# VectorE makes one GELU chunk in each of six groups of the first MoE as well

## The chip, the cores and the metric

The kernel runs on one core of a Trainium2 chip, as one launch. The metric is device time in microseconds (us). The profile names the core's engines PE (TensorE, matmuls; PEld are its weight loads), ACT (ScalarE), DVE (VectorE), POOL (GpSimd) and SP (SyncE, which issues DMAs).

## The reference

Attention over spatially pooled keys, followed by a feed-forward layer ("MoE" in the code) with a quick GELU:

```python
kv_pool = kv.reshape(B, H // r, r, W // r, r, C).mean(axis=(2, 4))
kv_flat = kv_pool.reshape(B, -1, C) @ w_sr
k = v = kv_flat
scale = 1.0 / np.sqrt(C)
s = scale * (q @ k.transpose(0, 2, 1))
s = s - s.max(-1, keepdims=True)
a = np.exp(s)
a /= a.sum(-1, keepdims=True) + 1e-09
x = (a @ v).reshape(B * S, D)
h = x @ w_in
g = h * (1.0 / (1.0 + np.exp(-1.702 * h)))
out = g @ w_out
```

q is 4 x 12288 x 128, kv is 4 x 384 x 32 x 128, r is 4, so each batch has 768 pooled keys. w_in is 128 x 2048, w_out 2048 x 128. All 49152 tokens pass through both parts.

## The kernel before, in words

**Tiles.** The tokens are cut into 96 groups of 512 (NG = 96). In attention a group has JC = 6 *chunks*, one for each 128 keys; in the MoE it has FCH = 16 chunks, one for each 128 hidden units. A chunk is a 128 x 512 tile of exponentials (attention) or of GELU values (MoE).

**Fill and drain.** Each chunk is made in a *fill* and used up in a *drain*. A fill is one matmul with 512 columns into a PSUM bank (L350 in attention, L596 in the MoE). ScalarE then turns three banks at a time, a *triple* of 1536 columns, into bf16 values (L352 Exp, L598 GELU) in a large SBUF tile `ag` of 102 chunk slots, handed out in frames of K = 3. A drain of attention is four times one matmul of 129 columns (L363: the values and the sum of weights). A drain of the MoE is one matmul of 512 columns (L606), sixteen of which add up in one bank. Because `ag` holds 102 chunks, the drains may run far behind the fills.

**Banks.** Six of the eight PSUM banks hold two triples by turns. The other two, 6 and 7, are accumulators (`acc()`) which attention's outputs, a MoE group's outputs and single extra fills take by turns. VectorE empties them: a reciprocal and a multiply for attention (L386, L389, into `x`), a transpose for a MoE group (L617, after which SP writes the output, L619).

**Rounds.** There are R = 2 rounds: attention for groups 0 to 47, MoE for groups 0 to 47 (here "the first MoE"), attention for 48 to 95, MoE for 48 to 95 ("the second MoE"). In the trace the first MoE's fills run from 140 to 485 us, its drains from 158 to 501 us. `x` holds one round; it is turned around by way of DRAM (`put_away`, `bring_back`, on SP's queue).

**Chunks that VectorE makes.** Some chunks bypass ScalarE. TensorE fills them singly into an accumulator bank (`early_fill`, L415 for attention and L409 for the MoE), and VectorE evaluates the function by a polynomial, instruction by instruction (`early_exp`, L431 to L444; `lent_gelu`, L453 to L475). There are three lists:

- `rolling`: single exponentials of attention, groups 10, 38 and 44 in the first round and 57, 63, ... in the second;
- `early`: all 24 exponentials of groups 48 to 51, made during the first MoE, from its group 12 on (`low`), into the lowest slots of `ag`;
- `lent`: the last chunk (number 15) of 17 groups of the second MoE.

Chunks of `rolling` and `lent` go into the small tile `aside` with K = 3 slots, taken by turns in the order in which the chunks are made. `early_todo` is that order; only its head is ever started. `raw`, the scratch for a lent chunk, is a slot of the pool of transposed queries (`qpool`, four buffers).

**The order of the work** is written out by a planner in Python, from L793 on. It keeps a clock of TensorE (`now`, in units of one 512-column matmul), one of VectorE (`dve`) and the expected ends of ScalarE's triples (`end`). Between one fill and the next it places, in this order: a step of a VectorE chunk, if VectorE's clock is not far ahead (`dve <= now + 2.0`, L807); a new VectorE chunk (L810), not during the last drains of a MoE group (`near`) and not unless `early_fits`; else drains, until the next fill is due. `early_fits` lets a lent chunk start when a group at most two before its own is being filled (L490) and when its slot of `aside` has been used up. A MoE group's drains don't start before its lent chunk is made, by the planner's clock (L840, L841):

```python
or (kind == "m" and first_of and (i, FCH - 1) in lent
    and made.get((i, FCH - 1), 1e9) > now + 1.0)
```

The order so fixed is each engine's program; the waits on the chip are semaphores.

**Background work.** `background(i)` runs when attention group i is first filled, `background_moe(g)` likewise for the MoE. They issue query loads (`load_qT`, by the dictionary `TURN`: group -> query tile), transposes of x, and the keys of batches 2 and 3, which are summed by accumulating DMAs on POOL's queue (`add_kv`, L173, each behind a `gate()` that VectorE sets) and then pass through VectorE and TensorE (`use_kv`; L179, L186, L193, L201) at groups 12 and 14, and 34 and 36, of the first MoE.

Of the kernel before, what the change touches and what calls it, by code (L numbers as in the profile page):

```python
# [7 lines left out]
F32 = mybir.dt.float32  # L8
F32R = mybir.dt.float32r
I32 = mybir.dt.int32  # L10
BF = mybir.dt.bfloat16
# [13 lines left out]
def kernel(  # L25
# [10 lines left out]
    FCH = d_ff // 128  # L36
    scale = 1.0 / (C ** 0.5)
    G = 512
    SG = 4 * G
    NG = B * N // G  # L40
    NS = NG // 4
    GB = NG // B
    SB = NS // B
    K = 3
# [24 lines left out]
    qpool = ctx.enter_context(tc.tile_pool(name="qpool", bufs=4))  # L69
# [15 lines left out]
    def acc(key=None):  # L85

        nonlocal last_acc
        last_acc = next_acc()
        turns.append(last_acc)
        turns.remove(last_acc)  # L90
        if key:
            closes[last_acc] = key
        return banks[:, last_acc, :]
# [24 lines left out]
    kv_tiles, kv_sums, pooled, pTs, kTs, vs = {}, {}, {}, {}, {}, {}  # L118
# [86 lines left out]
    qTs = {}  # L205
# [6 lines left out]
    def load_qT(s):  # L212
        qTs[s] = qpool.tile([128, 1, SG], BF, name="qT")
        nc.vector.memset(qTs[s][:, 0, 0:1], 0.0)
        nc.sync.dma_start_transpose(out=qTs[s], in_=q_bf[s * SG:(s + 1) * SG, :])


    QS = 3
# [7 lines left out]
    turned = set()  # L226
# [46 lines left out]
    for m in range(0, 128, 32):  # L273
        p = slice(m, m + 32)
# [30 lines left out]
    low = 0  # L305
# [23 lines left out]

    early = range(NG // R, NG // R + EARLY)  # L330
    rolling = [(i, JC - 1) for i in [10, *range(38, NG // R, 6), *range(57, 90, 6)]]
    lent = [(g, FCH - 1) for g in range(52, 94) if g % 5 in (2, 4)]
    aside = agpool.tile([128, K, 512], BF, name="aside")

    def weights(c):
        if c[0] == "a" and c[1] in early:
            return ag[:, (c[1] - early[0]) * JC + c[2], :]
        if c[0] == "a" and c[1:] in rolling:
            return aside[:, rolling.index(c[1:]) % K, :]
        if c[0] == "m" and c[1:] in lent:  # L340
            return aside[:, (len(rolling) + lent.index(c[1:])) % K, :]
        return ag[:, slot_of[c], :]


# [56 lines left out]
    COEFFS = (1.0000001192092896, -0.6931469440460205, 0.24022120237350464, -0.05550713464617729, 0.009675541892647743, -0.001327647129073739)  # L401

    def early_fill(i, jc):
        nonlocal steps, raw
        ps = acc()
        if (i, jc) in lent:
            if raw is None:
                raw = qpool.tile([128, 1, SG], BF, name="qT")[:, 0, 0:2 * G].bitcast(F32)
            nc.tensor.matmul(ps, w_in_sb[:, jc * 128:(jc + 1) * 128],  # L409
                             x[:, i % (4 * XS) * G:(i % (4 * XS) + 1) * G], start=True, stop=True)  # L410
            steps = lent_gelu(ps, weights(("m", i, jc)))
            early_step()
            return
        rhs = qTs[i // 4][:, 0, (i % 4) * G:(i % 4 + 1) * G]
        nc.tensor.matmul(ps, kTs[i // GB][:, jc * 128:(jc + 1) * 128], rhs, start=True, stop=True)  # L415
        steps = early_exp(ps, weights(("a", i, jc)))
        early_step()

    def early_step():
        nonlocal steps  # L420
        on_dve(next(steps))
        if steps.gi_frame.f_locals["last"]:
            steps = None
            made[early_todo.pop(0)] = dve
# [23 lines left out]
    def lent_gelu(ps, out):  # L448
        last = False
        a = npool.tile([128, 512], F32, name="ea", bufs=1)  # L450
        b = npool.tile([128, 512], F32, name="eb", bufs=1)
        e = npool.tile([128, 512], I32, name="ee", bufs=1)
        nc.vector.tensor_scalar_mul(raw, ps, -1.702 / LN2)  # L453
        yield 3.5
        nc.vector.tensor_scalar(a, raw, -126.0, 127.0, MAX, MIN)
        yield 2.2
        nc.vector.tensor_scalar_add(b, a, MAGIC)
        yield 2.2
        nc.vector.tensor_scalar(e, b, MAGIC - 127.0, 2.0 ** 23, SUB, MUL)
        yield 2.2  # L460
        nc.vector.scalar_tensor_tensor(b, b, MAGIC, a, SUB, SUB)
        yield 3.5
        nc.vector.tensor_scalar_mul(a, b, COEFFS[5])
        yield 2.2
        for k in (4, 3, 2, 1):
            nc.vector.scalar_tensor_tensor(a, a, COEFFS[k], b, ADD, MUL)  # L466
            yield 3.5
        nc.vector.scalar_tensor_tensor(a, a, COEFFS[0], e.bitcast(F32), ADD, MUL)
        yield 3.5
        nc.vector.tensor_scalar_add(a, a, 1.0)  # L470
        yield 2.2
        for m in (0, 256):
            nc.vector.reciprocal(b[:, m:m + 256], a[:, m:m + 256])  # L473
            yield RECIPROCAL
        nc.vector.scalar_tensor_tensor(out, raw, -LN2 / 1.702, b, MUL, MUL)  # L475
        last = True
        yield 3.5

    raw = None
    made, used = {}, []  # L480
    steps, early_todo = None, [c for c in rolling if c[0] < early[0]]
    early_todo += [(i, jc) for i in early for jc in range(JC)]
    early_todo += [c for c in rolling if c[0] > early[-1]] + lent

    def early_fits(p, i, jc):
        if (i, jc) in rolling:
            group = seq[p][1][0][0] if seq[p][0] == "a" else seq[p][1][0][0] // (NG // R) * (NG // R) + NG // R - 1
            return (i // GB, jc) in vs and (i in turned or i // 4 in qTs and i // 4 - 1 <= group // 4 and i >= 4 * QS) and len(used) > rolling.index((i, jc)) - K
        if (i, jc) in lent:
            return seq[p][0] == "m" and seq[p][1][0][0] >= i - 2 and len(used) > len(rolling) + lent.index((i, jc)) - K  # L490
        return low and min(slot_of.values()) >= low and (2, JC - 1) in vs

    def early_waits(t):
# [12 lines left out]
    def bring_back(n, m):  # L506
        o = m * PART
        lo = n * XS * SG + o * T
        nc.sync.dma_start_transpose(out=x[:, o * T:(o + PART) * T].unsqueeze(1), in_=x_bf[lo:lo + PART * T, :])
# [6 lines left out]
    def gate():  # L516

        one = gate_tile[:, gates[0] % 8:gates[0] % 8 + 1]
        gates[0] += 1
        nc.vector.memset(one, 0.0)  # L520
        nc.gpsimd.memset(one, 0.0)  # L521

    TURN = {6: 3, 7: 4, 8: 5, 20: 6, 21: 7, 22: 8, 25: 9, 32: 10, 35: 11, 40: 12}
    CAST = {0: [5], 13: [6], 14: [7], 15: [8], 16: [9], 26: [10, 11], 27: [12]}
    CAST_MOE = {20: 13, 21: 14, 22: 15, 23: 16, 33: 17, 34: 18, 35: 19, 36: 20, 37: 21, 38: 22, 39: 23}

    def background(i):

        first_round = i < GB * 2
        s = TURN.get(i, NS) if first_round else i // 4 + 3 if i % 4 == 0 else NS  # L530
        if s < NS:
            load_qT(s)
        if i in CAST:
            gate()
            for s in CAST[i]:
                cast_q(s)
        if i in (10, 12):
            gate()
            for jc in range(i % 10 * 3 // 2, i % 10 * 3 // 2 + 3):
                load_chunk(1, jc)  # L540
        if 0 <= i - 16 < JC:
            extras.append((key_and_value, 1, i - 16))
        if 0 <= i - 15 < JC:
            extras.append((pool_chunk, 1, i - 15))
        if i in (28, 33, 38):
            put_away(0, (i - 28) // 5)
        if i in (31, 36, 41):
            bring_back(0, (i - 31) // 5)
        if i == 28:
            gate()  # L550
            nc.gpsimd.dma_start(out=w_in_sb, in_=moe_w_in)
        if i == 29:
            gate()
            nc.gpsimd.dma_start(out=w_out_sb, in_=moe_w_out.rearrange("(o p) c -> p o c", p=128))

    def background_moe(g):

        n, g = divmod(g, 4 * XS)
        m, odd = divmod(g - 9, 2)
        m += FIRST  # L560
        if n == 0 and FIRST <= m < RT // PART:
            (bring_back if odd else put_away)(n, m)
        g += n * 4 * XS
        nonlocal low
        if g == 12:
            low = EARLY * JC
            order[:] = [f for f in order if f >= low // K]
        if g in CAST_MOE:
            gate()
            cast_q(CAST_MOE[g])  # L570
        if g in (41, 42):
            load_qT(g - 28)
        if g == 43:
            background(early[0])
        for b, lo in ((2, 2), (3, 24)):
            if lo <= g < lo + 8:
                gate()
                add_kv(b, g - lo)
            if g in (lo + 10, lo + 12):
                use_kv(b, (g - lo - 10) // 2)  # L580
# [74 lines left out]
    seq, todo = [], []  # L655
    todo_early = [("a", t, a) for t in range(NT) for a in range(2) if (t // TS * TS + TS - 1) // 4 in early]
    for n in range(R):
        part = [c for c in chunks if c[0] // (NG // R) == n]
        while part:
            m = sizes.pop(0) if sizes else K  # L660
# [12 lines left out]
        while flat:  # L673
            m = K if len(flat) > sum(rest) else rest.pop(0)
# [83 lines left out]
    def on_dve(cost):  # L758
        nonlocal dve
        dve = max(dve, now + 1.0) + cost  # L760
# [36 lines left out]
    for n in range(len(seq)):  # L797
        fill(n + 2)
        jobs(n + 3)
        while True:  # L800
# [33 lines left out]
            kind, i, c = source[0]  # L834
# [21 lines left out]
            if kind == "a" and i // 4 in early:  # L856
                early_left -= 1
                if not early_left:
                    low = 0
# [33 lines left out]
```

## Time and profile before

| | |
|---|---|
| median of 3 runs | 948.41 us (948.23 to 948.77) |
| span of the profiled execution, first to last instruction | 946.7 us |
| ACT: idle in the whole span | 13 us (933.5 busy), most of it in the first 35 us |
| L598 ACTIVATE, 1536 columns | 1496 ns each, 501 of them |
| L596 and L606, 512 columns | 379 ns each by a modelled end |
| DVE busy, 160 to 240 us | 10.50 of 80 us |
| DVE busy, 240 to 480 us | 175.53 of 240 us |
| DVE busy, 640 to 920 us | 199.22 of 280 us |

The profile is of one execution; its span leaves out what lies before the first and after the last instruction. A line of a group reads: source line, engine, operation, tiles written and read, count, then busy time, mean length of one, and the idle time of the engine just before, with what ended it. Lengths overlap where an engine is pipelined: an ACTIVATE is recorded as 1496 ns long, while the next one starts earlier than that. The chain of waits is read from start, length, and what ran; consecutive instructions of a line are joined ("x3").

### The profile page before, as it was taken

The page shows a single profiled execution, that of the slowest core. Times are in us where ns is not written, and L with a number is a line of the kernel's source. Part 1 is how long each engine was busy: PE and PEld are TensorE (multiplying, and loading weights), DVE is VectorE, ACT ScalarE, POOL GpSimd, SP SyncE. Part 2 cuts the span into 40 slices and gives each one's busy share as a digit, 9 for nine tenths or more (in the row PEclk, how much of TensorE's full clock was granted, in tenths as well). Part 3 has the DMA queues.
Part 4 walks back from the last instruction along what each step waited for, and adds up shares of the span by engine and source line. Part 5 has one row for each costly group of instructions (what it writes and reads, how often), then busy time and mean ns, then how long its engine had stood idle before and what let it go on. Part 6 is the DMA issues. An engine that isn't in the chain of part 4 may idle for free.

```text
span 946.7 us, 15374 instructions
## 1 busy us (share of the span) xinstructions
PE 933.9 (99%) x6200; PEld 502.5 (53%) x6314; DVE 575.1 (61%) x1091; ACT 933.5 (99%) x709; POOL 66.5 (7%) x115
## 2 busy tenths in 40 slices
PE   8999999999999999999999999999999999999998
PEld 4677776444444444444446777744444444444444
DVE  5753653011678776667765765376767766777651
ACT  6999999999999999999999999999999999999998
POOL 3101001330000232000000000000000000000000
PEclk9999999999999999999999999999999999999999
DMA  9997943999867799865335683552222222222222
GB/s 210 195 207 168 181 92 52 130 163 170 164 117 114 119 147 119 127 99 87 56 58 105 138 170 84 119 123 42 36 39 40 38 41 34 44 34 45 34 45 46
DMA packets 372856, 95.46 MB, mean 101 GB/s; under 512 B 346720, under 2 KB 370400, under 8 KB 372320
## 3 DMA queue, kind: packets, MB, share of 16 engines
q1 hardware_dynamic: 344000, 62.36, 36.9%
q0 software_dynamic: 28512, 31.99, 22.3%
q8 instruction: 49, 0.80, 0.3%
q14 instruction: 23, 0.19, 0.1%
q10 hardware_dynamic: 272, 0.13, 0.0%
HBM read 52.49 MB, written 48.76 MB: 107 GB/s over the span
## 4 chain that ended last, share of the span: by engine, by line
PE 97%; ACT 1%; DMA 1%; issue 1%; DVE 0%; POOL 0%; POOLq 0%
PE banks L606 35%; PE banks L596 34%; PE banks L363 14%; PE banks L350 12%; ACT ag L352 1%; PE banks L415 1%; DMA x<-in_kv_dram 1%; PE banks L139 0%; PE banks L409 0%; PE banks L634 0%; PE banks L236 0%; POOL x L222 0%; PE banks L161 0%; PE banks L294 0%; PE banks L192 0%
## 5 line engine op out<-in xcount | busy, mean ns | idle before, releaser
L598 ACT ACTIVATE ag<-banks 128x1536 bf16<-128x1536 f32 (+1 forms) x509 | 681.1, 1489 | 0.0
L596 PE MATMUL banks<-x,w_in_sb 128*128 128x512 bf16 x1476 | 405.8, 379 | 1.7
L606 PE MATMUL banks<-ag,w_out_sb 128*128 128x512 bf16 x1477 | 402.6, 379 | 1.7
L352 ACT ACTIVATE ag<-banks 128x1536 bf16<-128x1536 f32 (+2 forms) x192 | 245.6, 1421 | 3.5 <-PE banks L236 2.3
L606 PEld LDWEIGHTS <-w_out_sb 128*128 128x128 bf16 x1520 | 148.3, 98 | 177.2 <-issue 0.2
L596 PEld LDWEIGHTS <-w_in_sb 128*128 128x128 bf16 x1519 | 147.1, 98 | 171.3 <-issue 0.7
L617 DVE STREAM_TRANSPOSE o_sb<-banks 128x512 f32<-128x512 f32 x95 | 68.1, 717 | 171.4 <-PE banks L606 166.9
L363 PEld LDWEIGHTS <-ag 128*128 128x128 bf16 x2268 | 145.5, 98 | 44.6 <-issue 0.3
L363 PE MATMUL banks<-v,ag 128*128 128x129 bf16 x2268 | 163.0, 220 | 0.2
L350 PE MATMUL banks<-qT,kT 128*128 128x512 bf16 x498 | 145.0, 379 | 3.5 <-ACT ag L352 0.5
L442 DVE SCALAR_TENSOR_TENSOR ea<-ea,eb 128x512 f32<-128x512 f32 x132 | 90.4, 685 | 3.7 <-DVE ea L442 0.7
L386 DVE RECIPROCAL rec<-banks 128x3 f32<-128x3 f32 x124 | 22.3, 180 | 85.3 <-PE banks L363 84.9
L389 DVE TENSOR_TENSOR x<-banks,rec 128x384 bf16<-128x384 f32 x124 | 69.1, 557 | 4.3
L350 PEld LDWEIGHTS <-kT 128*128 128x128 bf16 x543 | 45.8, 98 | 25.9 <-issue 2.0
L473 DVE RECIPROCAL eb<-ea 128x256 f32<-128x256 f32 x34 | 57.6, 1724 | 0.5
L466 DVE SCALAR_TENSOR_TENSOR ea<-ea,eb 128x512 f32<-128x512 f32 x68 | 46.5, 683 | 1.9
L173 POOL DMA_DIRECT2D kvs<-in_kv_dram x32 | 40.4, 1323 | 19.3 <-DMA kvs<-in_kv_dram 17.1
L431 DVE TENSOR_SCALAR ea<-banks 128x512 f32<-128x512 f32 x33 | 22.8, 692 | 29.6 <-PE banks L415 29.2
L521 POOL MEMSET gate_tile<- 1x1 f32 x38 | 3.4, 89 | 325.8 <-DVE gate_tile L520 325.8
L453 DVE TENSOR_SCALAR qT<-banks 128x512 f32<-128x512 f32 x17 | 11.8, 692 | 20.7 <-PE banks L409 20.6
L437 DVE SCALAR_TENSOR_TENSOR eb<-eb,ea 128x512 f32<-128x512 f32 x33 | 22.8, 691 | 0.9
L444 DVE SCALAR_TENSOR_TENSOR ag<-ea,ee 128x512 bf16<-128x512 f32 x24 | 16.6, 691 | 1.2
(83 smaller groups left out, 286.3 us busy)
## 6 DMA issues: line engine op xcount, KB each, us to landing
out_dram<-o_sb SPq DMA_DIRECT2D x380, 64.0 KB, 2.0
kvs<-in_kv_dram POOLq DMA_DIRECT2D x32, 384.0 KB, 6.3
q_bf<-in_q_dram POOLq DMA_DIRECT2D x21, 512.0 KB, 6.6
x_bf<-x SPq DMA_DIRECT2D x13, 768.0 KB, 5.6
x<-in_kv_dram POOLq DMA_DIRECT2D x11, 512.0 KB, 10.4
x_bf<-x SPq DMA_DIRECT2D x6, 384.0 KB, 4.6
x<-in_q_dram POOLq DMA_DIRECT2D x5, 256.0 KB, 15.3
x<-in_kv_dram SPq DMA_DIRECT2D x1, 1024.0 KB, 5.0
```

What stands on the lines that cost most here:

```text
L173: nc.gpsimd.dma_start(out=kv_sums[b][:, i2], in_=kv_p[b, i, w, :, i2], **({"accum_op": ADD} if n else {}))
L350: nc.tensor.matmul(ps[:, k, :], kTs[i // GB][:, jc * 128:(jc + 1) * 128], rhs, start=True, stop=True)
L352: nc.scalar.activation(place([("a",) + c for c in chunks]), ps, AF.Exp, scale=scale)
L363: nc.tensor.matmul(av_of[u][:, k * (C + 1):(k + 1) * (C + 1)], weights(("a", i, jc))[:, o:o + T], vs[i // GB][:, jc, 0:C + 1], start=(jc = ...
L389: nc.vector.tensor_tensor(to, ps[:, :, 0:C], rec.unsqueeze(2).broadcast_to([128, TS, C]), MUL)
L442: nc.vector.scalar_tensor_tensor(a, a, COEFFS[k], b, ADD, MUL)
L466: nc.vector.scalar_tensor_tensor(a, a, COEFFS[k], b, ADD, MUL)
L473: nc.vector.reciprocal(b[:, m:m + 256], a[:, m:m + 256])
L596: nc.tensor.matmul(ps[:, k, :], w_in_sb[:, fc * 128:(fc + 1) * 128], x[:, g % (4 * XS) * G:(g % (4 * XS) + 1) * G], start=True, stop=True)
L598: nc.scalar.activation(place([("m",) + c for c in chunks]), ps, AF.Gelu_apprx_sigmoid)
L606: nc.tensor.matmul(o_of[g], w_out_sb[:, fc, :], weights(("m", g, fc)), start=(fc == 0), stop=(fc == FCH - 1))
L617: nc.vector.transpose(o_sb, o_of.pop(g))
```

## The change

Six chunks are added to the front of `lent`: chunk 15 of groups 2, 4, 6, 8, 10 and 12 of the first MoE. They leave the triples of that MoE (762 chunks for ScalarE in place of 768) and are made in `early_todo` after the three `rolling` chunks of the first round and before the 24 `early` ones. The turns of `aside` get a list of their own, `turn`, in the same order. `raw` is now taken when attention group 40 is filled, given back at group 43 of the first MoE, and taken again for the second MoE; the load of query tile 12 moves from group 40 to group 42, which keeps the four buffers of `qpool` in step.

```diff
-    lent = [(g, FCH - 1) for g in range(52, 94) if g % 5 in (2, 4)]
+    lent = [(g, FCH - 1) for g in range(2, 13, 2)] + [(g, FCH - 1) for g in range(52, 94) if g % 5 in (2, 4)]
+    turn = [("a",) + c for c in rolling if c[0] < early[0]] + [("m",) + c for c in lent if c[0] < early[0]]
+    turn += [("a",) + c for c in rolling if c[0] > early[-1]] + [("m",) + c for c in lent if c[0] > early[-1]]
...
-        if c[0] == "a" and c[1:] in rolling:
-            return aside[:, rolling.index(c[1:]) % K, :]
-        if c[0] == "m" and c[1:] in lent:
-            return aside[:, (len(rolling) + lent.index(c[1:])) % K, :]
+        if c in turn:
+            return aside[:, turn.index(c) % K, :]
...
             if raw is None:
-                raw = qpool.tile([128, 1, SG], BF, name="qT")[:, 0, 0:2 * G].bitcast(F32)
+                new_raw()
...
+    def new_raw():
+        nonlocal raw
+        raw = qpool.tile([128, 1, SG], BF, name="qT")[:, 0, 0:2 * G].bitcast(F32)
...
+    early_todo += [c for c in lent if c[0] < early[0]]
     early_todo += [(i, jc) for i in early for jc in range(JC)]
-    early_todo += [c for c in rolling if c[0] > early[-1]] + lent
+    early_todo += [c for c in rolling + lent if c[0] > early[-1]]
...
-            return seq[p][0] == "m" and seq[p][1][0][0] >= i - 2 and len(used) > len(rolling) + lent.index((i, jc)) - K
+            return seq[p][0] == "m" and seq[p][1][0][0] >= i - 2 and len(used) > turn.index(("m", i, jc)) - K
...
-    TURN = {6: 3, 7: 4, 8: 5, 20: 6, 21: 7, 22: 8, 25: 9, 32: 10, 35: 11, 40: 12}
+    TURN = {6: 3, 7: 4, 8: 5, 20: 6, 21: 7, 22: 8, 25: 9, 32: 10, 35: 11, 42: 12}
...
+        if i == 40:
+            new_raw()
...
         if g == 43:
+            raw = None
             background(early[0])
```

More of the change, by code (lines that the diff above doesn't have):

```diff
@@ L403, in early_fill @@
     def early_fill(i, jc):
-        nonlocal steps, raw
+        nonlocal steps
         ps = acc()
@@ L487, in early_fits @@
             group = seq[p][1][0][0] if seq[p][0] == "a" else seq[p][1][0][0] // (NG // R) * (NG // R) + NG // R - 1
-            return (i // GB, jc) in vs and (i in turned or i // 4 in qTs and i // 4 - 1 <= group // 4 and i >= 4 * QS) and len(used) > rolling.index((i, jc)) - K
+            return (i // GB, jc) in vs and (i in turned or i // 4 in qTs and i // 4 - 1 <= group // 4 and i >= 4 * QS) and len(used) > turn.index(("a", i, jc)) - K
         if (i, jc) in lent:
-            return seq[p][0] == "m" and seq[p][1][0][0] >= i - 2 and len(used) > len(rolling) + lent.index((i, jc)) - K
+            return seq[p][0] == "m" and seq[p][1][0][0] >= i - 2 and len(used) > turn.index(("m", i, jc)) - K
         return low and min(slot_of.values()) >= low and (2, JC - 1) in vs
@@ L563, in background_moe @@
         g += n * 4 * XS
-        nonlocal low
+        nonlocal low, raw
         if g == 12:
```

## Prediction

> **What bounds the kernel now.** I read the page's busy shares first, then the groups of instructions, then the chain inside the first MoE, then the counts of weight loads by stretch, because the first two can't decide between TensorE and ScalarE. From the page:
>
> ```profile
> span 946.7 us, 15374 instructions
> ...
> PE 933.9 (99%) x6200; PEld 502.5 (53%) x6314; DVE 575.1 (61%) x1091; ACT 933.5 (99%) x709; POOL 66.5 (7%) x115
> ...
> L598 ACT ACTIVATE ag<-banks 128x1536 bf16<-128x1536 f32 (+1 forms) x509 | 681.1, 1489 | 0.0
> L596 PE MATMUL banks<-x,w_in_sb 128*128 128x512 bf16 x1476 | 405.8, 379 | 1.7
> L606 PE MATMUL banks<-ag,w_out_sb 128*128 128x512 bf16 x1477 | 402.6, 379 | 1.7
> ```
>
> ScalarE's GELU line (L598) has no idle time before it. TensorE's two MoE lines have 1.7 us each, but their 379 ns are modelled ends, so "busy" could hide a wait of some 160 ns before each matmul. Start times can't hide it. This is the chain of waits in a stretch of the first MoE:
>
> ```profile
> 163.40 0.65 PE banks L596 x3
> 164.04 0.65 PE banks L606 x3
> 164.69 0.65 PE banks L596 x3
> ...
> 166.63 0.86 PE banks L606 x4
> 167.50 0.65 PE banks L596 x3
> ...
> 171.38 0.65 PE banks L596 x3
> 172.03 0.86 PE banks L606 x4
> ```
>
> From 163.40 to 172.03 the unabridged chain holds 40 matmuls of 512 columns: 8.63 / 40 = 0.2158 us from start to start. Whether three or four drains (L606) stand between two fills (L596), it is the same spacing; a TensorE that waited for ScalarE would show gaps ahead of the fills. Now the count. Weight loads, one a matmul, in the window 160 to 240 us, where this change puts most of its work:
>
> ```profile
> L606 PEld LDWEIGHTS <-w_out_sb 128*128 128x128 bf16 x189 | 18.5, 98 | 22.3
> L596 PEld LDWEIGHTS <-w_in_sb 128*128 128x128 bf16 x180 | 17.5, 98 | 20.7
> L184 PEld LDWEIGHTS <-pooled 96*128 96x128 bf16 x4 | 0.3, 97 | 0.2
> L199 PEld LDWEIGHTS <-pT 128*128 128x128 bf16 x3 | 0.3, 98 | 0.2
> L192 PEld LDWEIGHTS <-w_sr_sb 128*128 128x128 bf16 x1 | 0.1, 98 | 0.1
> ```
>
> 369 x 0.2158 = 79.6 us and about 0.5 us for the eight small ones: 80.1 of 80 us. The same sum for 240 to 480 us (535 + 526 + 24 wide loads, 72 of the 129-column kind at 0.057, 24 small) gives 239.8 of 240, and for 640 to 920 us, in the second MoE with its lent chunks, (658 + 625 + 15) x 0.2158 = 280.1 of 280. Over the whole trace I added up by how much each step from one weight load to the next exceeds the usual one for its shape: after 60 us this comes to 0.65 us in all, no single step over 0.11 us. Before 60 us it is about 10 us, the start-up, which the change doesn't reach. So TensorE is full from 60 us to the last matmul. ScalarE is full as well, by the windows view:
>
> ```profile
> 160.00:240.00 80.00, 79.58 (x370) 36.51 (x377) 10.50 (x23) 80.00 (x61) 19.02 (x20) 1.00 1.09 151
> ...
> 640.00:920.00 280.00, 278.63 (x1273) 126.87 (x1298) 199.22 (x274) 280.00 (x210) 0.00 (x0) 1.00 0.25 39
> ```
>
> The columns are PE, PEld, DVE, ACT, POOL, then the granted clock (1.00). VectorE has 10.5 of 80 us of work where the new chunks go. ScalarE is at 80.00: two engines are saturated together, and freeing one of them frees nothing unless the other also gets less.
>
> **Part by part.** *Removed from ScalarE:* 6 chunks leave the triples of the first MoE, 768 - 6 = 762 = 254 triples in place of 256. From 158.72 us, 31 ACTIVATEs take 41.91 us: (41.91 - 1.50) / 30 = 1.347 us from one to the next, so ScalarE loses 2 x 1.347 = 2.69 us of work.
>
> *TensorE:* six fills move from L596 to the early fill's matmul, with the same weights, tokens and 512 columns, and the six drains stay. Its work changes by 0. Since TensorE is late everywhere, the 2.69 us turn into ScalarE waiting. All that could be won is the 0.65 us of stalls; I count 0, and keep -0.65 us as the end of the range.
>
> This is where the Trainium skill speaks for a gain. "Perfetto Trace Analysis" (Identifying the Most-Contended Engine) says to judge TensorE by the share of weight-load time and the others by occupancy; here that is 53% against ScalarE's 99%, so ScalarE would bound and the change would win its 2.69 us. "TensorE: Matmul & The Clock Gate" (Back-to-back issue gap) gives about 131 ns per 512-column matmul for a sustained stream; by that figure, as an estimate, TensorE would need 48 of the 80 us. This trace shows no 512-column step below 0.215 us, so I go by the trace.
>
> *VectorE:* one GELU chunk costs, by the rows of the second MoE, 0.692 (L453) + 4 x 0.427 (L455, L457, L459, L470) + 0.690 + 0.424 + 4 x 0.683 (L466) + 0.690 + 2 x 1.724 (L473) + 0.669 = 11.05 us. Six are 66 us. VectorE is idle for 69.5 us in 160 to 240 and 11.9 us in 140 to 160, so there is room, but little: the chunks come every second group. What hides them is the lead of fills over drains. Group 2 is filled from 155.4 us and its drain starts at 171.65 us; group 12 from 227.55 and 239.1. A chunk must be made before the planner lets its group's drain begin.
>
> The pace: in the second MoE a chunk takes 12.7 to 14.4 us from its first VectorE instruction to its last, 13.6 on average, with one or two evacuations (L617) inside, and 0.65 us more from its weight load. 14.3 us a chunk stands against two groups of drains, 2 x (239.07 - 158.27) / 12 = 13.47 us, so each chunk comes 0.8 us later against its group. The first may start when group 0 is filled, 140.3 us, and shares VectorE with the last attention normalisations until 158.8 us. An exponential in such company took 12.2 us, against 7.5 us in the MoE, 1.63 times as long. From 141.5 us: (158.3 - 141.5) / 1.63 = 10.3 of 13.6 us are done by 158.3, the rest by 162. That is 9.7 us before group 2's drain; five chunks later 9.7 - 5 x 0.83 = 5.5 us; the pooled keys of batch 2 (L179, L186, L193, L201) take 2.2 us of VectorE at 225 to 232 us, which leaves some 3.3 us for group 12. No drain is held: cost 0.
>
> *Small terms.* Each lent chunk borrows one of the two accumulator banks until L453 has read it. Of 17 such fills and 33 exponential fills in the trace, 7 show an extra step, 0.55 us together, the longest 0.108 us: six more cost 0 to 0.65 us; I take the mean, 0.55 us / 50 x 6, about 0.1 us. An evacuation may wait for a 1.72 us reciprocal, but the other bank has a whole group (6.7 us) to come free. ScalarE's pace beside a busy VectorE: 210 ACTIVATEs start in 280 us (1.333 us) in the second MoE, no slower. POOL's eight accumulating key loads wait for gates that VectorE sets; batch 3's loads have run beside a busy VectorE, and L179 waited for nothing there. The load of query tile 12 moves from group 40 to group 42: SP issued it at 118.45 us, then the transposed load of x at 122.56, then nothing until 165.47; its first reader is the exponential at 246.9 us. The order of the two swaps in an idle queue: cost 0. The 24 early exponentials start after the last lent chunk; they began at 246.9 us, after the keys of batch 2, and (12, 15) is made by about 236 us. If it were 3 us late, the last exponential, made at about 482 us, would still be before its drain at 487.08: cost 0, and if that cover were gone, a microsecond late is at most a microsecond.
>
> *Sum:* 946.7 + 0.1 = 946.8 us of span. The median, 948.41, lies 1.7 us above the span of the one profiled execution; I carry that over: **948.5 us**.
>
> **Rivals.** (A) *ScalarE is what bounds.* For it: no idle before L598, and 80.00 of 80. Against: the constant 0.2158 us with four drains in a row, and 80.1 us of matmuls in 80. It would give 948.4 - 2.7 = 945.7 us. Chance 0.03.
>
> (B) *A held drain, slower.* The planner doesn't open a group's drain until its lent chunk is made by its own VectorE clock. While it holds, TensorE only fills, 3 matmuls per 1.347 us where 6.24 fit: 52% of the hold is lost for good, since nothing later has slack. It decides from the point where the first chunk is made after 171.65 us, or a chunk takes over 13.47 + 9.7 / 5 = 15.4 us. If the first chunk starts only after the last normalisation (158.8), it is made at 173.1: held 1.5 us, then 0.83 more for each of five, and 2.2 for the keys: 7.8 us held, 4.1 lost: 952.5 us. For it: 14.3 against 13.47, and fills that allow no chunk to start in the last drains of a group. Against: the 17 chunks of the second MoE were made 10.1 us or more before their own drain, the last of sixteen, and so 3.6 us or more before their group's first. Chance 0.10.
>
> (C) *The order behind it.* The early exponentials slip past their drains at 487 us, or the shifted order puts a wait into the second half: 1 to 3 us, 951 us. Chance 0.03.
>
> That the chunks aren't moved can't be: they leave the triples' list, and would be missing.
>
> **The numbers.** Likeliest, 0.84: 948.5 us, own range 947.4 (stalls of 0.65 gone, 0.4 of scatter between runs) to 949.5 us. For 8 in 10 the range reaches into B and C up to 950.8 us. Within 0.2% (1.9 us, about what a measurement of this kernel can tell from no change) lies the likeliest case: 0.84. Faster 0.03 is A; slower 0.13 is B and C.
>
> **What would show it.** Right: in the changed profile the wide matmuls still start every 0.2158 us from 160 to 240 us; ScalarE has 2 activations fewer and idle time of about 2.7 us, ended by TensorE; VectorE's load in 160 to 240 rises from 10.5 to about 70 us; the lent drains come several us after L475. Wrong: fills with gaps ahead of them and runs of fills without drains between (B), late L363 drains around 490 us (C), or a span near 944 us with ScalarE still at 100% (A). What would make it wrong above all is a chunk slower than 15.4 us.

## The result and the profile after

The changed kernel takes 950.26 us (median of 18 runs, 950.15 to 950.52), the kernel before 948.56 us (18 runs, 948.18 to 948.80): a ratio of 1.0019, 95% interval 1.0012 to 1.0026. It is 1.7 us slower. That is inside the 1.9 us that the prediction counted as no change, but above the range of its likeliest case (947.4 to 949.5 us); only the part of the range that was added for the slower rivals B and C, up to 950.8 us, takes it in. The page of the changed kernel, whose lines from 419 on have moved (L596 is now L604, L606 is L614, L598 the activation is L606, L617 is L625):

```profile
span 948.4 us, 15584 instructions
...
PE 940.8 (99%) x6314; PEld 502.7 (53%) x6314; DVE 638.0 (67%) x1181; ACT 930.8 (98%) x707; POOL 67.0 (7%) x115
...
L606 ACT ACTIVATE ag<-banks 128x1536 bf16<-128x1536 f32 (+1 forms) x507 | 678.3, 1500 | 0.0
L604 PE MATMUL banks<-x,w_in_sb 128*128 128x512 bf16 x1513 | 409.3, 379 | 0.0
L614 PE MATMUL banks<-ag,w_out_sb 128*128 128x512 bf16 x1497 | 406.8, 379 | 0.0
```

ScalarE has two ACTIVATEs and 2.7 us of busy time less (930.8 against 933.5), VectorE 63 us more. The span grew by 1.7 us, from 946.7 to 948.4, as the medians did. TensorE's busy time can't be compared, since the profile of before had lost 114 matmul records and this one none; weight loads are 6314 in both. The windows view of the changed kernel (PE, PEld, DVE, ACT, POOL, clock):

```profile
160.00:240.00 80.00, 80.00 (x379) 36.40 (x377) 64.37 (x102) 80.00 (x61) 19.40 (x21) 1.00 1.07 153
...
640.00:920.00 280.00, 280.00 (x1298) 126.76 (x1296) 198.41 (x274) 280.00 (x210) 0.00 (x0) 1.00 0.26 39
```

VectorE went from 10.50 to 64.37 us between 160 and 240, where about 70 was forecast; TensorE made the same 377 weight loads there as before.

**Where the 1.7 us are.** I added up again by how much each step from one weight load to the next exceeds the usual one for its shape. After 60 us this was 0.65 us before and is 2.66 us now; the start-up is much the same (10.4 and 10.3 us), and from the last matmul's weight load to the end of the span it is 3.6 and 3.4 us, so that 1.7 of the 2.0 us are left in the span. The 2.0 us of new waits are of two kinds. *Waits for an accumulator bank* that VectorE has not emptied: 0.436 us at 141.6, 0.467 at 941.5, and nine small steps after single fills; 1.66 us in all against 0.55. *Waits ahead of a fill*, for ScalarE to be done with the triple two places earlier: 0.153 and 0.176 us at 143.8 and 158.6, 0.155 at 404.3, 0.35 together at 550 to 565, a few of 0.03; 0.95 us against 0.06.

The largest two can be read in the trace. Weight loads of the changed kernel at the switch to the first MoE:

```profile
140.67 0.10 PEld L409 LDWEIGHTS <-w_in_sb 128*128 128x128 bf16 x1
140.88 0.77 PEld L363 LDWEIGHTS <-ag 128*128 128x128 bf16 x10
142.04 0.49 PEld L363 LDWEIGHTS <-ag 128*128 128x128 bf16 x8 [0.40 <-issue]
```

and the chain of waits there:

```profile
141.04 0.23 PE banks L409
141.28 0.02 issue
141.30 0.70 DVE qT L457
142.00 0.04 issue
142.04 0.67 PE banks L363 x9
```

The first lent chunk (2, 15) is filled by L409 right behind the first triple of the MoE and takes one of the two accumulators. Nine attention matmuls complete the output in the other; the tenth begins a new output and needs the borrowed bank, and VectorE's first instruction (L457, 0.70 us) is still reading it. The other large wait is in the last drains:

```profile
940.61 0.10 PEld L614 LDWEIGHTS <-w_out_sb 128*128 128x128 bf16 x1
940.82 0.76 PEld L642 LDWEIGHTS <-ag 128*128 128x128 bf16 x10
942.01 1.04 PEld L642 LDWEIGHTS <-ag 128*128 128x128 bf16 x18 [0.43 <-issue]
```

The last group (L642) uses four banks; one of them still holds group 94 until its transpose (L625, at 941.24) is through. Before, the profile had two fills ahead of these drains and more pairs among them, and no wait:

```profile
938.12 0.34 PEld L596 LDWEIGHTS <-w_in_sb 128*128 128x128 bf16 x2
938.58 0.88 PEld L634 LDWEIGHTS <-ag 128*128 128x128 bf16 x12
939.41 0.15 PEld L596 LDWEIGHTS <-w_in_sb 128*128 128x128 bf16 x2
```

### The profile page after: what moved, and what is told of

It reads as the page before. It is cut to its first block, busy times and chain, and to the rows that moved or that the text cites. A ratio compares the mean times of both kernels' runs of the same rounds, so it can differ in the third digit from the quotient of the medians.

```text
span 948.4 us, 15584 instructions
## 1 busy us (share of the span) xinstructions
PE 940.8 (99%) x6314; PEld 502.7 (53%) x6314; DVE 638.0 (67%) x1181; ACT 930.8 (98%) x707; POOL 67.0 (7%) x115
## 4 chain that ended last, share of the span: by engine, by line
PE 97%; ACT 1%; DMA 1%; DVE 0%; issue 0%; SPq 0%; POOL 0%; POOLq 0%
PE banks L604 34%; PE banks L614 34%; PE banks L363 14%; PE banks L350 12%; ACT ag L352 1%; DMA x<-in_kv_dram 1%; PE banks L415 1%; PE banks L409 1%; PE banks L139 0%; PE banks L642 0%; DMA out_dram<-o_sb 0%; DVE o_sb L625 0%; SPq L627 0%; POOL x L222 0%; PE banks L161 0%
## 5 line engine op out<-in xcount | busy, mean ns | idle before, releaser
L606 ACT ACTIVATE ag<-banks 128x1536 bf16<-128x1536 f32 (+1 forms) x507 | 678.3, 1500 | 0.0
L604 PE MATMUL banks<-x,w_in_sb 128*128 128x512 bf16 x1513 | 409.3, 379 | 0.0
L614 PE MATMUL banks<-ag,w_out_sb 128*128 128x512 bf16 x1497 | 406.8, 379 | 0.0
L614 PEld LDWEIGHTS <-w_out_sb 128*128 128x128 bf16 x1520 | 148.6, 98 | 178.3 <-issue 0.7
L604 PEld LDWEIGHTS <-w_in_sb 128*128 128x128 bf16 x1513 | 146.4, 98 | 168.7 <-issue 0.7
L350 PE MATMUL banks<-qT,kT 128*128 128x512 bf16 x543 | 148.5, 379 | 1.5 <-DVE kT L163 0.4
L625 DVE STREAM_TRANSPOSE o_sb<-banks 128x512 f32<-128x512 f32 x95 | 67.7, 713 | 109.8 <-PE banks L614 101.0
L446 DVE SCALAR_TENSOR_TENSOR ea<-ea,eb 128x512 f32<-128x512 f32 x132 | 90.5, 686 | 3.2
L477 DVE RECIPROCAL eb<-ea 128x256 f32<-128x256 f32 x46 | 78.4, 1726 | 0.7
L470 DVE SCALAR_TENSOR_TENSOR ea<-ea,eb 128x512 f32<-128x512 f32 x92 | 63.1, 686 | 2.6
L457 DVE TENSOR_SCALAR qT<-banks 128x512 f32<-128x512 f32 x23 | 15.9, 691 | 28.3 <-PE banks L409 27.9
## 6 DMA issues: line engine op xcount, KB each, us to landing
x<-in_kv_dram POOLq DMA_DIRECT2D x11, 512.0 KB, 10.3
x<-in_q_dram POOLq DMA_DIRECT2D x5, 256.0 KB, 15.4
```

Source lines behind the costliest of these rows:

```text
L350: nc.tensor.matmul(ps[:, k, :], kTs[i // GB][:, jc * 128:(jc + 1) * 128], rhs, start=True, stop=True)
L604: nc.tensor.matmul(ps[:, k, :], w_in_sb[:, fc * 128:(fc + 1) * 128], x[:, g % (4 * XS) * G:(g % (4 * XS) + 1) * G], start=True, stop=True)
L606: nc.scalar.activation(place([("m",) + c for c in chunks]), ps, AF.Gelu_apprx_sigmoid)
L614: nc.tensor.matmul(o_of[g], w_out_sb[:, fc, :], weights(("m", g, fc)), start=(fc == 0), stop=(fc == FCH - 1))
L625: nc.vector.transpose(o_sb, o_of.pop(g))
```

## The experiments

Theory 1: TensorE is full from 60 us on, ScalarE as well, so ScalarE's relief is worth nothing, and the loss is the waits that the planner's new order makes on TensorE. Rival 1: ScalarE bounds, its relief is worth 2.7 us, and something else takes more. Rival 2: VectorE's 66 us of new work cost, by late evacuations, the same for each chunk. "Before" stands beside each group of runs at 948.4 to 948.5 us.

**Less work, in the order of the kernel before.** Three runs leave work out.

```diff
-        nc.scalar.activation(place([("m",) + c for c in chunks]), ps, AF.Gelu_apprx_sigmoid)
+        to = place([("m",) + c for c in chunks])
+        n = 2 if len(chunks) == K and chunks[0][0] in LESS and chunks[0][1] < K else len(chunks)
+        nc.scalar.activation(to[:, 0:n, :], ps[:, 0:n, :], AF.Gelu_apprx_sigmoid)
...
-        nc.tensor.matmul(o_of[g], w_out_sb[:, fc, :], weights(("m", g, fc)),
-                         start=(fc == 0), stop=(fc == FCH - 1))
+        if not (2 <= g < 38 and fc == 7):
+            nc.tensor.matmul(o_of[g], w_out_sb[:, fc, :], weights(("m", g, fc)),
+                             start=(fc == 0), stop=(fc == FCH - 1))
```

ScalarE alone (the first edit, `LESS = range(2, 38, 2)`):

> The kernel before, with the same order on every engine, but in 18 triples of the first MoE (one in every second group from 2 to 36) ScalarE evaluates 1024 of the 1536 columns; the third chunk is left out. ScalarE has 18 x 0.427 = 7.7 us less to do, TensorE and VectorE the same. Theory 1 (TensorE is full, freeing ScalarE alone gives nothing): 948.5 us, within -0.7 and +0.2. Rival (ScalarE bounds, the change should have gained and lost it elsewhere): 948.5 - 7.7 = 940.9 us.

TensorE alone (the second edit):

> The kernel before, but one drain matmul is left out in each of groups 2 to 37 of the first MoE: TensorE has 36 x 0.2158 = 7.8 us less to do, ScalarE the same. Both engines full: ScalarE's own pace now bounds, 948.5 us less what ScalarE's triples have over their shortest spacing of 1.331 us in that stretch, at most some 2 us: 946.5 to 948.5. TensorE alone bounds: 940.8 us. ScalarE alone bounds: 948.5 us.

Both:

> The kernel before with both omissions, 18 thirds of a triple on ScalarE and 36 drains on TensorE. Both engines full: now the time falls by about the whole 7.7 us, to 941 us. Each theory in which one engine alone bounds gives about 941 us as well, but then one of the other two runs must have given it already.

Measured: ScalarE less, 948.33 us (ratio 0.9999, 0.9990 to 1.0009); TensorE less, 948.38 us (1.0000, 0.9991 to 1.0009); both less, 944.36 us (0.9957, 0.9944 to 0.9971). Taking 7.7 us from ScalarE wins nothing, which ends rival 1; taking 7.8 us from TensorE wins nothing either. The windows of the run with less on ScalarE show it idle beside a TensorE that made as many weight loads (376) as before (377):

```profile
160.00:240.00 80.00, 80.00 (x378) 36.46 (x376) 10.62 (x23) 78.56 (x61) 19.01 (x20) 1.00 1.09 154
```

and the chain of the run with less on TensorE is, between 206 and 213 us, ScalarE alone, at 6.72 / 5 = 1.344 us a triple, no faster than before (counted from start to start between 160 and 240 us, 1.342 us here and 1.345 before):

```profile
205.95 6.72 ACT ag L598 x5
```

Both together won 4.0 us, not the 7.7 I had expected. In its trace TensorE's waits are 4.30 us, 3.65 more than before, and 7.77 - 3.65 = 4.1. Most of these waits (3.8 us) stand ahead of a fill: TensorE reaches it while ScalarE is still at work on the triple two places earlier. My reading, which no run tests by itself, is that the places don't match: the ScalarE thirds were left out in every second group and the drains in every one, and two triples of banks are all the slack there is between the two engines, so that work taken from one in one place isn't made good elsewhere.

**The moved query load alone.** The changed kernel with the front of `lent` empty:

```diff
-    lent = [(g, FCH - 1) for g in range(2, 13, 2)] + [(g, FCH - 1) for g in range(52, 94) if g % 5 in (2, 4)]
+    lent = [] + [(g, FCH - 1) for g in range(52, 94) if g % 5 in (2, 4)]
```

> The changed kernel without its six chunks: only the scratch slot taken at attention group 40 and the query load moved from group 40 to 42 are left. If the loss comes with the chunks: 948.5 us, within 0.3. If the moved load or the reordered buffers cost: up to 950.3 us.

Measured: 948.43 us (1.0001, 0.9992 to 1.0010), waits 0.64 us. The move costs nothing; the loss comes with the chunks.

**Three of the six.** `range(2, 13, 2)` becomes `range(2, 7, 2)`, or `range(8, 13, 2)`.

> Only chunk 15 of groups 2, 4 and 6 goes to VectorE in the first MoE. Theory 1 (TensorE is full; the 1.8 us are the waits seen in the trace: 0.72 at the switch to the MoE at 141 to 159 us, 0.47 in the last drains at 941 us, 0.3 in the second attention, 0.15 at 404 us): the wait at the switch stays whole, the others shrink or stay, 949.2 to 949.9 us. Rival 2 (each chunk costs the same, by VectorE's 66 us of new work in the way of evacuations): half, 949.3 us. Rival 1 (ScalarE's relief is worth 1.3 us and something else costs more): not told apart here.

> Only chunk 15 of groups 8, 10 and 12. Theory 1: no wait at the switch, because no chunk is made beside the attention's last drains; with ScalarE half as far ahead the last drains wait less: 948.4 to 949.0 us. Rival 2 (the same cost for each chunk): 949.3 us, as much as the first three.

Measured: the first three alone, 950.79 us (1.0025, 1.0015 to 1.0034), slower than all six; the last three alone, 949.48 us (1.0011, 1.0002 to 1.0020). Both missed my figures, by 0.9 and 0.5 us, and both for one reason: each list gives a new order with waits of its own. The first three kept the wait at 141.6 us (0.435) and the one at the end (0.467), and met a new one at the switch to the second attention, again a borrowed bank right before a drain needs it:

```profile
485.09 0.23 PE banks L415
485.32 0.02 issue
485.34 0.70 DVE ea L435
486.04 0.04 issue
486.08 0.81 PE banks L614 x3
```

0.60 us went there. The last three have none at 141 us, as expected, but 0.34 us of waits for ScalarE at 520 to 535 and the 0.47 at the end. The loss is not so much a chunk: rival 2 has its first point against it.

**Six given, six taken back.** The second MoE's list becomes `g % 5 == 4 or g in (62, 77, 92)`.

> The six new chunks stay, six of the second MoE's seventeen go back to ScalarE (11 are left: groups 54, 59, 62, 64, 69, 74, 77, 79, 84, 89, 92), so that ScalarE has as much to do as in the kernel before. Theory 1: the wait at the switch stays; ScalarE is no longer ahead of TensorE at the end, so the 0.47 us in the last drains go: 949.3 to 949.9 us. If ScalarE's relief were worth something, giving it back would cost 2.7 us: 952.9 us.

Measured: 950.34 us (1.0019, 1.0010 to 1.0028). Giving 2.7 us of work back to ScalarE cost nothing, as theory 1 has it. My reason for the wait in the last drains fell, though: with ScalarE as busy as before, it is still there.

```profile
940.53 0.31 PEld L614 LDWEIGHTS <-w_out_sb 128*128 128x128 bf16 x2
940.96 0.76 PEld L642 LDWEIGHTS <-ag 128*128 128x128 bf16 x10
942.15 0.93 PEld L642 LDWEIGHTS <-ag 128*128 128x128 bf16 x16 [0.43 <-issue]
```

Here too the last group's drains follow those of group 94 without a fill between. So the wait goes with the order in which fills and drains end, not with how far ahead ScalarE is; why the planner's order ends so was not looked into.

**The last drains.** They leave the bank that is still being emptied alone for seven chunks in place of three:

```diff
-        parts = [(m, fc) for m in range(4) if m != held or fc > 2]
-        if fc == 2:
-            parts += [(held, f) for f in range(3)]
+        parts = [(m, fc) for m in range(4) if m != held or fc > 6]
+        if fc == 6:
+            parts += [(held, f) for f in range(7)]
```

> The changed kernel, but the last group's drains leave the accumulator bank that VectorE is still emptying alone for seven chunks in place of three, 21 quarter drains (1.2 us) in place of 9 (0.5 us). Theory 1: the wait of 0.47 us at 941 us goes and the time with it, 949.8 us. If that wait is a record's fault, or is made up for elsewhere: 950.3 us.

Measured: 949.74 us (1.0013, 1.0004 to 1.0022), 0.52 us less than the changed kernel. All 64 quarter drains now run in one piece:

```profile
942.72 3.77 PEld L642 LDWEIGHTS <-ag 128*128 128x128 bf16 x64
```

**VectorE's work left out.** In the six new chunks all instructions but the first and the last are skipped (thirteen of the fifteen; the expectation below counts two too many); the last one then reads `raw` twice.

> The changed kernel in the same order, but of the GELU polynomial of the six new chunks VectorE runs only the first and the last instruction (the fifteen between are left out): some 58 of the 66 us of new VectorE work are gone, the six single fills and the borrowed banks stay. Theory 1 (the loss is waits made by the new order on TensorE): 950.0 to 950.3 us, the waits at 141.5 and 941 us unchanged. Rival 2 (VectorE's new work costs, by late evacuations): about 948.6 us.

Measured: 950.27 us (1.0019, 1.0009 to 1.0028), the changed kernel's time, with 17.75 us of VectorE's work between 160 and 240 in place of 64.37, and the same 2.66 us of waits:

```profile
140.86 0.10 PEld L409 LDWEIGHTS <-w_in_sb 128*128 128x128 bf16 x1
141.07 0.77 PEld L363 LDWEIGHTS <-ag 128*128 128x128 bf16 x10
142.24 0.49 PEld L363 LDWEIGHTS <-ag 128*128 128x128 bf16 x8 [0.39 <-issue]
```

That ends rival 2. The polynomial behind its first instruction is free; where the single fills stand among the other matmuls is not.

**ScalarE's work left out, in the new order.** The edit of the first run, with `LESS = range(0, 38, 2)`, and the like in `fill_attn` for groups 70 to 83.

> The changed kernel in the same order, but ScalarE evaluates 1024 of 1536 columns in 19 triples of the first MoE (groups 0 to 36) and in about 14 of the second attention (groups 70 to 83); those thirds are left out. Theory 1, second half: TensorE's waits before fills at 144, 159, 404 and 550 to 565 us are for ScalarE, which is late there by the new order although it has less to do in all; 0.88 us of waits go: 949.3 to 949.7 us. The waits for accumulator banks (141.5, 941 us) stay. If those waits have another cause: 950.3 us. If ScalarE bounded as a whole: 14 us less, 936 us.

Measured: 949.63 us (1.0013, 1.0004 to 1.0021), 0.63 us less than the changed kernel for 14 us of work left out. The waits at 143.8 and 158.6 us are gone, that at 404 fell from 0.155 to 0.057, those at 550 to 565 from 0.35 to 0.03. At 563.6 us a wait of 0.13 us came in place of one of them, ahead of a drain (L365) that starts when VectorE's first instruction of a chunk (here L437) ends, at 563.5. The two large bank waits stayed at 0.434 and 0.467. Around 158.6 us, the changed kernel and then this run, where the three loads ahead of fills (L604, here L607) take 0.37 us again in place of 0.54:

```profile
157.91 0.71 PEld L363 LDWEIGHTS <-ag 128*128 128x128 bf16 x9
158.57 0.54 PEld L604 LDWEIGHTS <-w_in_sb 128*128 128x128 bf16 x3
```

```profile
157.80 0.71 PEld L365 LDWEIGHTS <-ag 128*128 128x128 bf16 x9
158.47 0.37 PEld L607 LDWEIGHTS <-w_in_sb 128*128 128x128 bf16 x3
```

So the waits ahead of fills are for ScalarE: it has less to do in all, and is late in places.

**A later start.** With the edit of the last drains, and a new chunk starting only when the group just before its own is being filled:

```diff
-            return seq[p][0] == "m" and seq[p][1][0][0] >= i - 2 and len(used) > turn.index(("m", i, jc)) - K
+            return seq[p][0] == "m" and seq[p][1][0][0] >= i - (1 if i < 48 else 2) and len(used) > turn.index(("m", i, jc)) - K
```

> The changed kernel with the last drains as in the run before (seven chunks in place of three), and a new chunk may start only when the group before its own is being filled, so that the first is not filled right at the switch to the MoE. Theory 1: the 0.5 us at the end go and the 0.75 us around the switch go or shrink, 949.0 to 949.4 us; whatever the new order brings, the time is 948.5 us plus the waits of the weight loads beyond 0.65 us, within 0.3. A version that beats the kernel before is not to be had this way: no wait, no loss, and no gain.

Measured: 954.60 us (1.0065, 1.0052 to 1.0077). My 949 was far off. Weight loads of this run:

```profile
213.29 0.10 PEld L614 LDWEIGHTS <-w_out_sb 128*128 128x128 bf16 x1
213.51 0.10 PEld L604 LDWEIGHTS <-w_in_sb 128*128 128x128 bf16 x1
214.01 0.53 PEld L604 LDWEIGHTS <-w_in_sb 128*128 128x128 bf16 x3 [0.40 <-issue]
215.35 0.53 PEld L604 LDWEIGHTS <-w_in_sb 128*128 128x128 bf16 x3 [0.82 <-issue]
216.69 0.31 PEld L604 LDWEIGHTS <-w_in_sb 128*128 128x128 bf16 x2 [0.82 <-issue]
```

Fills without a drain between, at ScalarE's pace: this is rival B of the prediction, the held drain. It comes before groups 8, 10 and 12 and costs 4.7 of the run's 6.82 us of waits. The chunk of group 8 was made at 215.2 us, but group 8's drains begin at 217.3: the planner's clock for VectorE is slower than the engine. Its costs for a lent chunk add up to 55.4 units of 0.2158 us, 11.96 us, where the instructions take 11.05. What the run changed for the good (no wait at 141 us, none at the end) can't be seen beside it.

**One sum for all.** In every run, time = 948.4 us + TensorE's waits after 60 us in the profiled execution - 0.65, less TensorE work left out. The span of an execution is the sum of its steps, so the table shows that the time went into waits and nowhere else; what each wait was for is shown by the traces and runs above.

| kernel | waits, us | sum, us | measured, us |
|---|---|---|---|
| before | 0.65 | 948.4 | 948.56 |
| ScalarE less | 0.64 | 948.4 | 948.33 |
| TensorE less (7.77 us) | 8.59 | 948.6 | 948.38 |
| both less (7.77 us) | 4.30 | 944.3 | 944.36 |
| load alone | 0.64 | 948.4 | 948.43 |
| last three | 1.91 | 949.7 | 949.48 |
| ScalarE less, new order | 1.96 | 949.7 | 949.63 |
| last drains | 2.17 | 949.9 | 949.74 |
| changed | 2.66 | 950.4 | 950.26 |
| VectorE less, new order | 2.66 | 950.4 | 950.27 |
| six swapped | 2.52 | 950.3 | 950.34 |
| first three | 3.27 | 951.0 | 950.79 |
| later start | 6.82 | 954.6 | 954.60 |

The sum holds within 0.25 us over a span of 10 us. For "last drains" I left out a wait of 1.97 us in its profiled execution, at 951.59 us the only one of eleven above 949.8: its accumulating key loads ran late, the last could be issued only at 218.7 us and landed at 228.1 (218.3 in the changed kernel), and L179 waited for it. No version tried that does the same work beats the kernel before, and by the sum a new order can win 0.65 us after the start-up at most.

## Why the prediction was right, and where it was not

- *What bounds*: right, and now shown rather than argued. TensorE still makes its 377 loads in 160 to 240 us; ScalarE's relief is worth 0.0 us by the first run and again by the six swapped. The rule of the Trainium skill weighed there ("Perfetto Trace Analysis", Identifying the Most-Contended Engine) points to ScalarE by 98 to 99% of occupancy against 53% of weight-load time on TensorE (the page names MFU as a second measure for TensorE, which was not worked out here); the first run, 7.7 us less on ScalarE for 0.0 us of time, speaks against it here. The same skill's spacing for back-to-back matmuls, some 131 ns at 512 columns ("TensorE: Matmul & The Clock Gate", Back-to-back issue gap), is not seen in any run; where nothing waits, the loads of the wide matmuls keep to 215 or 216 ns.
- *ScalarE 2.69 us less, VectorE 66 us more, TensorE unchanged*: right (2.7 and 63 us in the profile; 6314 weight loads in both). ScalarE's last GELU of the kernel ends 2.9 us earlier (939.15 against 942.06) while TensorE's last weight load comes 1.8 us later (944.97 against 943.12).
- *The query load moved, cost 0*: right, 948.43 us without the chunks.
- *The lead of fills over drains*: the outcome right, the reckoning not. The first chunk took 20.2 us beside the attention, against the 20.5 reckoned from 141.5 to 162, and was made at 161.5. The chunks of groups 2 to 12 were made 12.5, 10.8, 10.7, 7.3, 6.2 and 1.9 us before their group's first drain; I had 9.7 for the first and 3.3 for the last. No drain was held, but that was partly luck. From one chunk made to the next I had 14.3 us and had named 15.4 as the limit; it was 15.4 on average over the first four steps, and 18.8 in the last, which the keys share. The middle four chunks took 13.3 to 14.3 us from their weight load, as reckoned, but only the third started right behind the one before. So the chunk of group 12 was made at 242.1 us, not by 236. It came in time because group 12's first drain had moved from 239.1 to 244.05 us in the new order, which I had not foreseen; at its old time it would have been held for 3 us.
- *The small terms, about 0.1 us*: wrong, and this is the step that missed. They came to 2.0 us. I priced the borrowed bank by the mean of 50 fills, 0.011 us each, with 0.108 as the longest; at the switch, where attention drains take a bank every 1 to 2 us, one cost 0.436. And I took TensorE's order for given but for the six matmuls, though the planner lays out everything after 140 us anew: 0.95 us of waits for ScalarE and 0.47 at the end came from that.
- *Rivals*: A is out. B didn't occur. Its price was somewhat too high: in the last run 12.8 us between one group's last drain and the next one's first (4.0, 4.9 and 3.8, where 0.2 to 1.1 is usual) cost 4.7 us, 37% of the hold and not 52%. C, the order behind the change, "1 to 3 us", had 0.03 of the chance and is what happened, at 1.7 us, though also in the first half and at the end.
- *The number*: no gain was called from the ledger of start times, and that held. 948.5 us missed by 1.8, and the range held only by what B and C had added to it. To price a reshuffled order at some waits, not at none, would have put the number nearer.
- *A misread row*: the 210 ACTIVATEs in 280 us of the second MoE are all that overlap the window; 209 start in it, 1.344 us apart and not 1.333. That ScalarE is no slower there than beside an idle VectorE (1.345 us) stands.

## What to carry to other kernels

When two engines are both shown as full, add up one engine's start-to-start times before moving work off the other: relief of 7.7 us on one alone was worth 0.0 here, and on both 4.0. A borrowed bank or buffer is priced by the place where it is borrowed, not by a mean: the same fill cost 0 to 0.6 us, by whether the next user came within VectorE's first instruction. And where an order written by a planner has been freed of waits, adding chunks ahead of it gave a new order with new waits in each of the six versions tried (1.0 to 6.2 us); count them in the weight loads, and repair them one by one, as the 0.5 us in the last drains.

## What the runs showed that I had not expected

- TensorE and ScalarE were balanced to well under 1 us over groups 2 to 37 of the first MoE: with 7.7 us less on ScalarE, or 7.8 us less on TensorE, the time did not move by 0.2 us.
- Reading the activation pace: with TensorE waiting, ScalarE's triples of 1536 columns still started 1.342 us apart (160 to 240 us), so the 1.345 us of the kernel before was within 0.003 us of its own pace.
- The switch from Exp to GELU costs ScalarE one table load of 1.28 us and no more: in the changed kernel it starts at 141.24 and the first GELU at 142.53 us.
